# A fused linear attention and mixture of experts: row scatters are no longer ordered behind the early reads of the first two experts

## Chip, cores and metric

One core of a Trainium2 chip. The metric is the device time of one execution in microseconds. The kernel is written in Tile: the program names tiles and operations, and the framework derives from them which instruction has to wait for which. Engine names in the profile: PE is TensorE (matmuls; PEld its weight loads), DVE VectorE, ACT ScalarE, POOL GpSimd, SP SyncE, which here only issues DMAs.

## What is computed

A gated linear recurrence over 768 tokens for 4 x 8 heads of width 48, and behind it a mixture of 8 experts in which every one of the 4 x 768 = 3,072 tokens goes to exactly one expert:

```
f = 1 / (1 + exp(-f_logit))
for t in range(S):                                  # S = 768
    state = f[:, :, t, :, None] * state + einsum('bhd,bhe->bhde', k[:, :, t], v[:, :, t])
    y[:, :, t] = einsum('bhd,bhde->bhe', q[:, :, t], state)
x = y.transpose(0, 2, 1, 3).reshape(3072, 384)
logits = x @ w_gate                                 # (3072, 8)
expert_idx = argmax(logits, axis=1)
gate_w = softmax(logits)[arange(3072), expert_idx]
for e in range(8):                                  # rows of expert e
    y[rows_e] = maximum(x[rows_e] @ w1[e], 0) @ w2[e]   # 384 -> 1024 -> 384
return gate_w[:, None] * y
```

All numbers are float32.

## The kernel before

**Two stages.** The first works through the recurrence in 12 units (NU = 12). A unit is one chunk of 128 tokens of two batches, with all heads. The second goes through the 8 experts, each with its w1 and w2, 1.5 MB each.

**Between the stages lies a buffer in device memory**, `xs`, with a region of rows for each expert. A row has 400 floats (1,600 bytes): the token's 384 values, its number (TOK) and its weight (GATE). As soon as the tokens of a unit are known, each is written into the next free row of its expert. That is a scatter (L189): an indirect DMA issued by POOL, 128 rows at a time, whose row numbers come from a tile `posi`.

**How a row finds its place.** `rows` (L663) multiplies a unit's outputs `ys` with a matrix that both turns them to row layout and gives the gate's logits. `lay` (L688, L693) copies the rows from PSUM to a tile `xr`. Two units at a time form a group, up to units 8 and 9; units 10 and 11 stand alone. For each group a `Route` does: `choose` (DVE, L214 to L222: which expert), `count` (PE, L226 and L227: how many before this one, into `rp`), `place` (DVE, L233 to L251: the row numbers `posi`, read from `rp`), `weigh` (ACT, L254), `fill` (DVE, L258 to L260: the gate's weight into `xr`), and `send` (POOL, the scatters: four for a group of two units, two for a single unit).

**The order of the loop** over n = 1 to 13 (L803) is written out by hand. Within one n the unit `here` = n is scored (L543) and masked (DVE, L549), the unit before it gets its outputs (L571 within the chunk, L592 from the state), and the unit two back is settled (ACT, L633, a copy from PSUM into the single buffer `ys`) and put into rows (L663). While the loop still has units ahead, scatters are handed out two at a time (`sends`, `scatter_some`). Near the end they go out at once: those of units 6 and 7 near the end of n = 10, after `place` and `fill`; those of units 8 and 9 in n = 12; those of unit 10 in n = 12; those of unit 11 in n = 13.

**Early reads.** At n = 10 (NU - 2), before the scatters of units 6 and 7 in program order, `load_rows` reads the first 128 rows of experts 0 and 1 (EARLY = 2) from `xs`: for each, four DMAs of blocks (`load_blocks`, L273) into a tile `xrow` and one (L285) of token numbers and weights into `tg`, all issued by SP. PE begins with these two experts while the last units' routing is still going on: `turn_early` transposes the rows (DVE, L299), `widen` (PE, L316, in three parts: 3, 4 and 1 of 8 blocks, into banks that the trace calls `s`) multiplies with w1, with the relu on ACT (L326) or DVE (L328), and `narrow` (PE, L332, into `yp`) with w2, behind which the results are scaled (L343) and scattered to the output. The rows that are read must have been written by then. Whether the first 128 rows of both experts are full is tested when units 4 and 5 are placed (`settled`, the tile `lack`); if one is not, a general path behind the main program does the rows again. With these inputs it does not run.

**What orders the scatters.** The framework treats `xs` as one tensor: a scatter may write any row, so it would wait for all earlier scatters and reads of `xs`. Between scatters that is switched off: each is declared free of the group "xs" and joins it (`declare_no_dep`, `add_to_no_dep_group`), since no row is written twice. The early reads are in no such group. A read waits for the scatters issued before it, and a scatter issued after the reads waits until they have landed.

**Behind the loop** SP writes padding rows (`load_pads`) and reads the remaining rows of the experts; both come after the last scatters.

Of the kernel before, what the change touches and what calls it, by code (L numbers as in the profile page):

```python
# [19 lines left out]
C = 128  # L20
# [35 lines left out]
BK = 32  # L56
# [6 lines left out]
TOK, GATE, USED, ROW = DM, DM + 1, DM + 2, DM + 16  # L63
# [62 lines left out]
def kernel(  # L126
# [15 lines left out]
    nc = tc.nc  # L142
# [13 lines left out]
    xs = nc.dram_tensor("xs", (ROWS + T, ROW), F32, kind="Internal").ap()  # L156
# [28 lines left out]
    nc.gpsimd.memset(pad, 0.0)  # L185
    nc.gpsimd.memset(pad[:, TOK : TOK + 1], float(FAR))

    def scatter(dst, idx, src, bound, group=None):
        ins = nc.gpsimd.indirect_dma_start(  # L189
            out=dst,  # L190
            out_offset=bass.IndirectOffsetOnAxis(ap=idx, axis=0),
            in_=src,
            in_offset=None,
            bounds_check=bound,
            oob_is_err=False,
        ).ins
        if group:
            tc.declare_no_dep(ins, group=group, reason="no row is written twice")
            tc.add_to_no_dep_group(group, ins)

    class Route:

# [59 lines left out]
        def send(self, chunks):  # L262
            for c in chunks:
                scatter(xs, self.posi[:, c : c + 1], self.xr[:, c, :], ROWS - 1, self.group)
# [4 lines left out]

    def load_blocks(to, rows):  # L270

        for j in range(128 // BK):
            nc.sync.dma_start(  # L273
                to[BK * j : BK * j + BK],
                rows[:, DB * j : DB * j + DB].rearrange("(i c) m -> c i m", c=BK),
            )

    def load_rows(row, count=C):

        rows = xs[ds(row, count)] if not isinstance(row, int) else xs[row : row + count]  # L280
        n, whole = -(-count // C), count // C
        x = rowp.tile([128, TILES * C // BK, DB], F32, name="xrow")[:, 0 : count // BK]
        tg = rowp.tile([128, TILES, USED - TOK], F32, name="tg")[:, 0:n]
        load_blocks(x, rows)
        nc.sync.dma_start(  # L285
            tg[:, 0:whole], rows[0 : whole * C, TOK:USED].rearrange("(t p) r -> p t r", p=C)
        )
        if n > whole:
            nc.sync.dma_start(tg[0 : count - whole * C, whole], rows[whole * C :, TOK:USED])
        return {"n": n, "rows": count, "x": x, "tg": tg}  # L290

    def turn(x, pool=None):

# [47 lines left out]
    def put(x, t, yp, group):  # L341
        ysb = ep.tile([128, DM], F32, name="ysb")
        nc.vector.tensor_scalar(ysb, yp, x["tg"][:, t, 1:2], None, op0=OP.mult)  # L343
        scatter(out, x["dst"][:, t : t + 1], ysb, N - 1, group)
# [13 lines left out]
    def put_half(x, t, h, yp, group):  # L358
        ysb = ep.tile([128, HD], F32, name="ysh")
        nc.vector.tensor_scalar(ysb, yp, x["tg"][:, t, 1:2], None, op0=OP.mult)  # L360
        scatter(out_halves, x["dst2"][:, h : h + 1], ysb, 2 * N - 1, group)
# [30 lines left out]
    def load_expert(e):  # L392

        t = int(e < EARLY)
        x = load_rows(first[e] + t * C, int(FIXED[e]) - t * C)
        if e in RIDE:
            rows = xs[ds(slot(0, RIDE[e], NONE), T)]
            nc.sync.dma_start(x["tg"][C - T :, TILES - 1], rows[:, TOK:USED])
        return x
# [21 lines left out]
    with ExitStack() as st:  # L421
# [46 lines left out]
        whole, ab = slice(0, SEG), (slice(0, HP), slice(HP, SEG))  # L468
# [132 lines left out]
        def added(u):  # L601

            x = units[u]
            x["dp"] = turns("dp", [128, SEG, D])
            for a in range(2):
                for p, h, r in heads():
                    s = HP * a + p
                    nc.tensor.matmul(  # L608
                        x["dp"][r, s],
                        lhsT=x["kn"][:, s, r],  # L610
                        rhs=x["v"][:, a, 2 * p + h],
                        start=s == 0,
                        stop=True,
                        skip_group_check=True,
                    )

        def update(u):

            x = units[u]
            new = wk.tile([128, SEG, D], F32, name="state", bufs=4)  # L620
            last = _bc(x["last"], 2, D)
            if x["old"] is None:
                nc.vector.tensor_copy(new, x["dp"])
            else:
                nc.vector.tensor_tensor(new, x["dp"], x["old"], op=OP.add)
            states[u % 2] = new
            return lambda: nc.gpsimd.tensor_tensor(new, new, last, op=OP.mult)
# [7 lines left out]
        group = {}  # L635
# [167 lines left out]
        for n in range(1, NU + 2):  # L803
# [20 lines left out]
                scatter_some(n)  # L824
            if n == NU - 2:
                soon = [load_rows(first[e]) for e in range(EARLY)]
            if n == 1:
                units[0]["old"] = None
                added(0)
                update(0)()  # L830
# [208 lines left out]
    with ExitStack() as st:  # L1039
# [4 lines left out]
        def quad_rows(q):  # L1044

            x = qp.tile([128, 4, DB], F32, name="qrow")
            quad = {"q": q, "n": 1, "rows": C, "x": x, "second": [None] * 4}
            if q != 0:
                quad["tg"] = qp.tile([128, 1, USED - TOK], F32, name="qtg")
            for g in range(4):  # L1050
                rows = xs[ds(slot(0, 4 * q + g, NONE), T)]
                load_blocks(x[:, g : g + 1], rows)
                if q != 0:
                    nc.sync.dma_start(quad["tg"][g * T : g * T + T, 0], rows[:, TOK:USED])
            return quad
# [85 lines left out]
        for e in range(E):  # L1141
            x, w = rows_of[e], weights[e]
# [32 lines left out]
    with tc.If(todo > 0):  # L1175

        flag = nc.values_load(badi[0:1, 0:1], min_val=0, max_val=1)
        with tc.If(flag > 0):
            with ExitStack() as st:
# [6 lines left out]
                ins = {x: gp.tile([128, S], F32, name=f"g{x}") for x in "qkf"}  # L1186
# [69 lines left out]
        with ExitStack() as st:  # L1256
            bank, narrow_late, psz = tile_pools(st)
            with tc.For_i(0, E) as e:
                w1t = wpool.tile([128, KD, F], F32, name="w1t")
                w2t = wpool.tile([128, NF, DM], F32, name="w2t")  # L1260
                for w, src, by in ((w1t, moe_w1, W1), (w2t, moe_w2, W2)):
                    nc.sync.dma_start(
                        w, src[ds(e, 1)].rearrange("o a b -> (o a) b").rearrange(by, p=128)
                    )
                end = ep.tile([1, 1], I32, name="end", bufs=1)
                nc.sync.dma_start(end, ends_of[0:1, ds(e, 1)])
                rows_to = nc.values_load(end[0:1, 0:1], min_val=0, max_val=ROWS - C)
                nc.sync.dma_start(xs[ds(rows_to, C)], pad)
                with tc.For_i(e * REGION + skip, rows_to, C) as at:
                    x = load_rows(at)  # L1270
                    turn(x)
                    x["hT"] = ep.tile([128, NF, C], F32, name="hT", bufs=1)
                    widen(x, (w1t, w2t), bank, range(NF))
                    narrow_late(x, 0, (w1t, w2t), None)
# [53 lines left out]
```

## Time and profile before

| | |
|---|---|
| six executions | median 400.96 us, 400.43 to 402.29 |
| the profiled execution | 403.07 us; its span from first to last instruction 401.3 us |
| PE busy | 383.6 us (96% of the span) |
| DVE, POOL, ACT busy | 169.6, 116.5, 103.1 us |
| moved by DMA | 95.05 MB, mean 237 GB/s |
| mean granted clock of TensorE | 0.982 |

The profile is one execution, recorded by the hardware. Times in the timeline count from the span's start in microseconds. A timeline row reads: start, length, engine, line, operation, output<-input, shape, number of instructions merged into it, and in brackets how long the engine was idle before it and what ended the wait (inferred from semaphores). `issue` is time in which the profile shows nothing that was waited for. The ends of matmuls are modelled, so a row's end on PE is when the matmuls should be done, and the start of the instruction that reads the result is when the result was handed over.

The first stage lasts until about 138 us, the experts from there to the end; up to 154 us the early rows of experts 0 and 1 are worked on.

### The profile page before, as it was taken

What the parts mean: (1) busy time and instruction counts of PE and PEld (TensorE: products, weight loads), DVE (VectorE), ACT (ScalarE), POOL (GpSimd) and SP (SyncE); (2) the same over time, 40 slices, a digit from 0 to 9 for tenths busy, and PEclk for the clock granted to TensorE, in tenths of its full rate; (3) what the DMA queues carried; (4) which work ended last, traced back from release to release, by engine and by line L of the source; (5) the groups of instructions that cost most, each with busy time, mean ns of one, the idle gap of its engine ahead of it and who ended that gap; (6) DMA issues with size and microseconds to landing.
All of it is one profiled execution on the core that took longest, in us unless ns stands there. A gap on an engine that the chain in (4) does not pass through costs nothing.

```text
span 401.3 us, 7727 instructions
## 1 busy us (share of the span) xinstructions
PE 383.6 (96%) x3062; PEld 270.7 (67%) x3062; DVE 169.6 (42%) x365; ACT 103.1 (26%) x190; POOL 116.5 (29%) x118
## 2 busy tenths in 40 slices
PE   7898999999995999999999999999999999999993
PEld 7887898998985787777555555664556556554452
DVE  6899987989751352203112113113612113111350
ACT  6898877775431100000010010010000000001000
POOL 4378868788517120010100100100100100100011
PEclk9999999999998699999999999999999999999997
DMA  8999657779954147959339899989145349993231
GB/s 283 381 355 371 212 199 265 234 210 343 399 143 163 41 154 211 316 139 305 88 130 353 233 376 392 277 339 339 44 157 187 103 147 394 396 415 137 52 147 42
DMA packets 51516, 95.05 MB, mean 237 GB/s; under 512 B 20824, under 2 KB 40731, under 8 KB 49424
## 3 DMA queue, kind: packets, MB, share of 16 engines
q1 hardware_dynamic: 48016, 84.76, 62.5%
q0 software_dynamic: 3168, 9.64, 6.4%
q8 instruction: 25, 0.41, 0.4%
q14 instruction: 19, 0.16, 0.1%
q10 hardware_dynamic: 288, 0.08, 0.1%
HBM read 79.46 MB, written 15.21 MB: 236 GB/s over the span
## 4 chain that ended last, share of the span: by engine, by line
PE 87%; DMA 3%; DVE 2%; issue 2%; another core or an unknown queue 1%; POOL 1%; ACT 1%; SPq 0%; POOLq 0%; DVEq 0%; ACTq 0%
PE hps L316 27%; PE yps L332 23%; PE yps L1107 7%; PE xp L663 6%; PE s L543 4%; PE yt L571 4%; PE s L316 3%; PE hps L1081 3%; PE yp L332 3%; PE yt L592 3%; DMA f<-in_fu_dram 2%; PE kp L558 2%; PE dp L608 2%; DMA k<-in_ku_dram 1%
## 5 line engine op out<-in xcount | busy, mean ns | idle before, releaser
L316 PE MATMUL hps<-xT,w1t 128*128 128x352 f32 (+2 forms) x384 | 110.1, 447 | 0.0
L316 PEld LDWEIGHTS hps<-xT,w1t 128*128 128x128 f32 x384 | 72.7, 190 | 37.2 <-issue 1.9
L332 PE MATMUL yps<-w2t,hT 128*128 128x384 f32 x288 | 94.4, 487 | 0.0
L189 POOL DMA_INDIRECT out_dram<-ysb,dst x24 | 23.3, 972 | 225.2 <-DVE ysb L343 215.6
L332 PEld LDWEIGHTS yps<-w2t,hT 128*128 128x128 f32 x288 | 54.6, 190 | 38.6 <-issue 1.5
L326 ACT ACTIVATE hT<-hps 128x352 f32<-128x352 f32 (+2 forms) x28 | 13.7, 490 | 200.7 <-PE hps L316 171.9
L328 DVE TENSOR_SCALAR hT<-hps 128x352 f32<-128x352 f32 (+2 forms) x28 | 15.6, 558 | 93.0 <-PE hps L316 93.0
L343 DVE TENSOR_SCALAR ysb<-yps,tg 128x384 f32<-128x384 f32 x22 | 13.6, 618 | 74.4 <-PE yps L332 55.7
L189 POOL DMA_INDIRECT xs<-xr,posi x24 | 33.3, 1388 | 26.9 <-DVE ex L222 12.7
L549 DVE COPY_PREDICATED at<-mpack,s 128x512 f32<-128x512 uint8 x48 | 31.1, 729 | 6.2 <-PE s L543 6.2
L509 POOL TENSOR_TENSOR k<-k,r 128x1024 f32<-128x1024 f32 (+1 forms) x12 | 26.5, 2213 | 19.8 <-ACT r L505 10.4
L491 DVE TENSOR_TENSOR_SCAN sum<-g,cap 128x1032 f32<-128x1032 f32 (+1 forms) x14 | 28.8, 2060 | 3.5 <-ACT g L484 3.5
L663 PE MATMUL xp<-fpack,ys 128*128 128x104 f32 x192 | 26.4, 288 | 4.0 <-ACT ys L633 2.9
L663 PEld LDWEIGHTS xp<-fpack,ys 128*128 128x128 f32 x192 | 23.5, 197 | 6.1 <-ACT ys L633 3.2
L1107 PE MATMUL yps<-qw,hqT 128*32 128x192 f32 (+1 forms) x192 | 27.5, 381 | 0.2 <-issue 0.2
L543 PE MATMUL s<-q,k 64*128 64x128 f32 x384 | 24.7, 278 | 1.7 <-POOL last L527 1.1
L571 PE MATMUL yt<-at,v 128*48 128x128 f32 x384 | 25.1, 276 | 0.0
L543 PEld LDWEIGHTS s<-q,k 64*128 64x128 f32 x384 | 22.4, 188 | 3.6 <-issue 1.5
L571 PEld LDWEIGHTS yt<-at,v 128*48 128x48 f32 x384 | 20.0, 123 | 2.6 <-issue 1.5
L1107 PE MATMUL yps<-w2t,hT 128*32 128x384 f32 x192 | 21.4, 487 | 0.0
L633 ACT COPY ys<-yt 128x512 f32<-128x512 f32 x24 | 12.9, 591 | 17.8 <-PE yt L592 11.8
L532 DVE TENSOR_TENSOR q<-q,g 128x1024 f32<-128x1024 f32 (+1 forms) x14 | 16.5, 1183 | 0.2 <-DMA q<-in_qu_dram 0.2
(114 smaller groups left out, 366.3 us busy)
## 6 DMA issues: line engine op xcount, KB each, us to landing
qw<-in_moe_w_dram SPq DMA_DIRECT2D x16, 1536.0 KB
w1t<-in_moe_w_dram SPq DMA_DIRECT2D x8, 1536.0 KB
w2t<-in_moe_w_dram SPq DMA_DIRECT2D x8, 1536.0 KB
k<-in_ku_dram SPq DMA_DIRECT2D x12, 512.0 KB
q<-in_qu_dram SPq DMA_DIRECT2D x12, 512.0 KB
f<-in_fu_dram SPq DMA_DIRECT2D x11, 512.0 KB
xs<-pad SPq DMA_DIRECT2D x8, 600.0 KB
v<-in_vu_dram SPq DMA_DIRECT2D x12, 384.0 KB
```

The costliest lines, as they stand in the source:

```text
L189: ins = nc.gpsimd.indirect_dma_start(out=dst, out_offset=bass.IndirectOffsetOnAxis(ap=idx, axis=0), in_=src, in_offset=None, bounds_check= ...
L316: nc.tensor.matmul(x["h"][:, f], lhsT=w[0][:, j, b * 128 : b * 128 + 128], rhs=x["xT"][:, j], start=j == 0, stop=j == KD - 1,)
L328: nc.vector.tensor_scalar(to, x["h"], 0.0, None, op0=OP.max)
L332: nc.tensor.matmul(yp, lhsT=x["hT"][:, f, t * C : t * C + C], rhs=w[1][:, f, :], start=f == 0, stop=f == NF - 1,)
L491: nc.vector.tensor_tensor_scan(x["sum"][:, part].rearrange("p s c -> p (s c)"), x["g"][:, part].rearrange("p s c -> p (s c)"), cap[:, part ...
L509: ins = on.tensor_tensor(k, k, units[u]["r"][:, part], op=OP.mult).ins
L532: nc.vector.tensor_tensor(q, q, x["dec"][:, part], op=OP.mult)
L543: nc.tensor.matmul(ps[h][:, p], lhsT=x["k"][r, s], rhs=x["q"][r, s], start=True, stop=True)
L549: nc.vector.copy_predicated(x["at"][:, a, h], _bc(causal, 1, HP), x["ps", a][h])
L571: nc.tensor.matmul(x["yt"][DP * (h ^ a) : DP * (h ^ a) + D, a, p], lhsT=x["v"][:, a, 2 * p + h], rhs=x["at"][:, a, h, p], start=p == 0, st ...
L663: nc.tensor.matmul(xp[:, p], lhsT=x["ys"][:, a, p], rhs=wx[:, p, 0:XW] if a else wx[:, p, E:WX], start=True, stop=True,)
L1107: nc.tensor.matmul(yp[r], lhsT=h[:, f, at : at + T], rhs=w[:, f, cols], start=f == 0, stop=f == NF - 1, skip_group_check=True,)
```

## The change

The scatters of group "xs" that come after the early reads are declared free of them. For this `load_blocks` and `load_rows` hand back their DMA instructions, these are put into a group "early", and `scatter` declares itself independent of that group. Nothing is reordered in the program, no instruction is added, and no buffer changes.

```diff
+    early_reads = []
+
     def scatter(dst, idx, src, bound, group=None):
         ins = nc.gpsimd.indirect_dma_start(
...
         if group:
             tc.declare_no_dep(ins, group=group, reason="no row is written twice")
             tc.add_to_no_dep_group(group, ins)
+        if group == "xs" and early_reads:
+            tc.declare_no_dep(
+                ins,
+                group="early",
+                reason="the early tiles' rows are full, or the general path does them again",
+            )
...
     def load_blocks(to, rows):
 
-        for j in range(128 // BK):
+        return [
             nc.sync.dma_start(
                 to[BK * j : BK * j + BK],
                 rows[:, DB * j : DB * j + DB].rearrange("(i c) m -> c i m", c=BK),
-            )
+            ).ins
+            for j in range(128 // BK)
+        ]
...
-        load_blocks(x, rows)
-        nc.sync.dma_start(
-            tg[:, 0:whole], rows[0 : whole * C, TOK:USED].rearrange("(t p) r -> p t r", p=C)
+        reads = load_blocks(x, rows)
+        reads.append(
+            nc.sync.dma_start(
+                tg[:, 0:whole], rows[0 : whole * C, TOK:USED].rearrange("(t p) r -> p t r", p=C)
+            ).ins
         )
...
-        return {"n": n, "rows": count, "x": x, "tg": tg}
+        return {"n": n, "rows": count, "x": x, "tg": tg, "reads": reads}
...
             if n == NU - 2:
                 soon = [load_rows(first[e]) for e in range(EARLY)]
+                early_reads.extend(ins for x in soon for ins in x["reads"])
+                for ins in early_reads:
+                    tc.add_to_no_dep_group("early", ins)
```

## The prediction

> **What bounds the kernel now.** I read the page first, then the chain of waits, then the timeline from 88 to 160 us engine by engine, then stages. The page says PE 383.6 of 401.3 us: TensorE nearly always has a matmul. Past the kernel's first 43 us, only the stage where the diff works is an exception. This is the chain there (start, length, what):
>
> ```profile
> 118.50 0.22 ACT ex L254
> 118.72 5.94 another core or an unknown queue
> ...
> 125.37 1.41 PE xp L663 x8
> 126.78 0.79 issue
> 127.57 2.00 PE xp L663 x8
> 129.57 0.25 PE s L316
> 129.82 0.52 issue
> ...
> 138.67 5.16 PE yp L332 x16
> ```
>
> From 138.51 (first L332 matmul in the timeline) to the end PE has no gap worth naming: the stage 138:154 below shows 16.00 busy of 16.00. So the end is 138.51 + 262.8 = 401.3, and only what moves 138.51 counts. The stages are start:end, length, busy time of PE, PEld, DVE, ACT, POOL, then granted clock, DMA share, GB/s:
>
> ```profile
> 107.00:118.00 11.00, 10.80 (x170) 9.81 (x160) 6.83 (x31) 4.36 (x11) 0.00 (x0) 1.00 0.76 247
> 120.00:128.00 8.00, 4.24 (x35) 3.91 (x33) 1.03 (x7) 1.07 (x2) 5.98 (x7) 0.97 0.40 154
> 128.00:138.00 10.00, 8.58 (x38) 7.83 (x38) 1.71 (x12) 1.62 (x5) 3.28 (x7) 0.51 0.21 82
> 138.00:154.00 16.00, 16.00 (x87) 11.98 (x87) 9.22 (x38) 0.60 (x1) 3.00 (x3) 1.00 0.45 141
> ```
>
> POOL does nothing from 107 to 118, then scatters without a pause; in those 8 us PE is half idle, and for the next 10 its clock is 0.51. What did PE wait for? The timeline, one line for each end of a hand-over:
>
> ```profile
> 118.93 1.09 PE L592 MATMUL yt<-q,state 48*48 48x128 f32 x32
> 120.19 0.38 PE L227 MATMUL rp<-oh,fpack 128*128 128x16 f32 x2
> 124.73 1.07 ACT L633 COPY ys<-yt 128x512 f32<-128x512 f32 x2 [6.01 <-remote]
> 126.80 0.17 DVE L234 COPY counts<-rp 128x16 f32<-128x16 f32 x1 [7.59 <-PE xp L663]
> 133.36 0.29 DVE L671 TENSOR_REDUCE lg<-xp 128x8 f32<-128x32 f32 x2 [5.04 <-PE s L316]
> ```
>
> L592 ends by its row at 120.02, yet its reader L633 starts at 124.73 (4.71 late); L227 ends at 120.57, its reader L234 starts at 126.80 (6.23); the second L663 group ends at 129.57, its reader starts at 133.36 (3.79). Six us earlier the same hand-overs took 0.13 (L592 to L633, 114.32 to 114.45) and 0.03 (L227 to L234, 114.89 to 114.92), and after the scatters 0.03 again (137.87 to 137.90). Late hand-overs begin with the first of ten back-to-back scatters and end 2.7 us after the start of the last:
>
> ```profile
> 106.07 0.15 POOL L655 MEMSET xr<- 128x56 f32 x1
> 118.89 0.99 POOL L189 DMA_INDIRECT xs<-xr,posi  x1 [12.67 <-DVE ex L222]
> 120.19 0.97 POOL L189 DMA_INDIRECT xs<-xr,posi  x1 [0.30 <-issue]
> ...
> 130.64 0.97 POOL L189 DMA_INDIRECT xs<-xr,posi  x1 [0.30 <-issue]
> ```
>
> Pairs of scatters earlier show it small: L608 ends at 98.81 during one of 97.99 to 99.09, and its reader L625 starts at 99.56, 0.75 late; the L592 beside it takes 1.43 against 1.09 elsewhere. I don't know the mechanism; that scatters cause it is an inference from this coincidence.
>
> **The change, part by part.** No instruction is added. *Removed:* POOL's wait for ten reads (eight L273, two L285; SP issues them from 111.12 to 116.70) before the first scatter of units 6 and 7; the 12.67 us in its row. The label names a DVE step; the wait instructions of L189 run from 116.4, when the reads land. Its data (L251, L260) are ready at 107.74, and the instruction itself carries the wait for these, so it can start at 108.0. The same wait in the scatters of units 8 to 11 is long satisfied: nothing. SP's own 10.6 us wait, before the reads, for scatters already sent, stays; it ends at 110.99 as now. *Moved:* four scatters, each one POOL instruction and 128 rows of 1,600 B, from 118.9 to 108.0. Nothing else of POOL stands behind them but the next scatters. The four of units 8 and 9 (ready at 116.59) no longer queue behind them; the pairs of units 10 and 11 wait for DVE anyway.
>
> *DMA collision.* The moved 4 x 0.205 = 0.82 MB now land while the reads run; at the 401 to 436 GB/s of 102 to 108 us that is 2.0 us, so the reads, used by the transpose L299 at 118.39, may come at 120.4. I price it at nothing, covered: in the chain below the choice ahead of L299 ends after 120.6. Without that cover it costs up to 2.0. Bounds: 0 and 2.0.
>
> *What the old waits cost in all.* With no late hand-over PE would do after 120.57: L316 x18 2.25 (to 122.7), L663 2.03, L316 x24 at 0.117 each 2.8, L226/L227 0.6, L316 x6 0.7, so L332 at 128.8 instead of 138.51: 9.7 us to win at most. DVE's choice (1.42, from 133.36 to 134.78) hides under the 2.8.
>
> *What the new place of the scatters costs.* Not shown by any row, so bounded: by pairs, 0.35 us of PE a pair, five pairs 1.8, gain 7.9; by the train of ten, 9.7 over ten scatters is 0.97 each, gain 0. Between them I take trains of four, nearest to neither, and work out the order of events, with a hold that starts about 1 us into a train and is released between 1.5 us (pairs: 97.99 to 99.56) and 2.7 us (ten: 130.64 to 133.36) after its last scatter begins:
> 1. Train one at 108.0, steps of 1.28, last begins 111.85: release 113.4 to 114.6. PE has queued work until 114.32 (scores, L663, L571, L592), so it loses nothing yet. Two of the four masks L549 (1.3 us) and the choice (L671 to L222, 1.6 of work) are late: L226 starts at 116.3 to 117.5 instead of 114.25. PE idles 2.0 to 3.2.
> 2. Counts 0.64, place and scale 1.67 (114.92 to 116.59), 0.8 to issue (139.49 to 140.30 for the last pair): train two from 119.4 to 120.6, last begins 123.2 to 124.4, release 124.7 to 127.1. PE meanwhile does L663, L571, L592 (4.9), counts, L316 x18 (2.25), until 124.7 to 125.9.
> 3. L633 0.6 after the release, L663 2.03: to 127.3 to 129.7. The pair of units 10 starts 2.5 after the release (place and scale 1.5, issue 1.0), so its hold comes after this result is handed over; the choice, 1.4, runs beside PE's 24 L316, which end at 130.1 to 132.5; then 0.6 and 0.8.
> L332 starts at 131.5 to 133.9, middle 132.7: 5.8 us earlier. Against the profiled execution (403.07, span 401.3 and 1.77 around it) that is 397.3; the median of six runs is 400.96, 2.11 less, so **395.2**, own range 394.0 to 396.4, to 400 where the clock drops for part of it.
>
> *A rule weighed: the clock.* The clock is 0.51 in 128:138, after PE gaps of 2.70 (122.67 to 125.37) and 1.06. The Trainium skill, "TensorE: Matmul & The Clock Gate", Part 1, says a largely idle window of about 3.4 us halves the clock. By that rule step 1's gap just misses a drop; if one came, the half-speed time would be bought as in the profile.
>
> *A rule that speaks against it: the port.* The row: a scatter of 94.65 took 3.03 us beside DVE's scan L491, one of 103.02 beside the masks L549 took 1.03. The Trainium skill, "DMA: Bandwidth & Descriptors", SWDGE vs HWDGE vs iDMA, says DVE locks GpSimd out of writing descriptors in its two-port mode. By the rule, if masks counted, train one would last 13.0 instead of 4.9, its last scatter would begin 6.2 later, and the estimate would be 401.4. From 108 to 118 DVE runs masks and small operations, no scan, so the row's 1.03 holds.
>
> **Rivals.** *The hold disappears* (391.3 to 393.1): split trains act like pairs, or like the single scatters after 145, beside which PE shows no gap. For it: earlier pairs; against it: eight of them still follow each other closely. *It only moves* (400.3 to 401.6): 0.97 a scatter wherever it stands, or a wait I don't see keeps POOL where it is. For it: the count of scatters is the same. *Slower* (402.3 to 406): train one now falls into the recurrence, where every step waits for the one before. If its hold on the masks leaves PE idle before L226 for more than the 3.8 us (2.70 + 1.06) that preceded the drop now, the clock halves for the 10.24 us it stayed down before, 5.1 lost, and reads late by 2.0 no longer have cover: 133.9 + 5.1 + 2.0 = 141.0, 2.5 later than now, 403.5; more holds in the chain than I counted make up the rest. Against it: 2.0 to 3.2 is less than 3.8.
>
> **Chances.** Forecast 0.41, hold gone 0.20, only moved 0.15, slower 0.24. About 0.3% (1.2 us) can be told from no change. Faster: 0.61 plus a little of the third, 0.63; same 0.12; slower 0.25. Range from the second case to the near half of the fourth: 390.8 to 402.8, beside the forecast's own 394.0 to 396.4.
>
> **What would show it.** Right: first scatter of units 6 and 7 near 108 with no long wait; trains of four; L592 to L633 still late near 124, by less; L332 first at 131.5 to 133.9; less time at 0.5 clock. Wrong: the first scatter still at 118; hand-overs prompt with scatters running (then they were never the cause); L299 late and PE waiting for it; a clock under 1 before 125.

## The result, and the profile after

| | before | after |
|---|---|---|
| median of the runs | 401.67 us (39 runs, 399.05 to 403.53) | 398.2 us (18 runs, 395.69 to 400.48) |
| ratio, 95% interval | | 0.9918 (0.9902 to 0.9933) |
| profiled execution, its span | 403.07, 401.3 | 397.74, 395.9 |
| mean granted clock of TensorE | 0.982 | 0.990 |

Faster by 0.8%, some 3.3 us, where 5.8 were forecast. 398.2 lies outside the forecast's own 394.0 to 396.4, inside its "to 400 where the clock drops for part of it" and inside the whole range of 390.8 to 402.8. In the changed kernel's trace the line numbers stand 2 to 12 higher: the scatter is L191, the outputs are L583 and L604, the copy to `ys` L645, the rows L675, `count` L234 and L235, `widen` L328, `narrow` L344.

The timeline of the changed kernel, POOL's scatters and the readers of PE's results:

```profile
107.69 0.99 POOL L191 DMA_INDIRECT xs<-xr,posi  x1 [1.78 <-DVE xr L268]
...
110.54 1.34 DVE L561 COPY_PREDICATED at<-mpack,s 128x512 f32<-128x512 uint8 x2 [0.93 <-PE xp L675]
111.55 0.97 POOL L191 DMA_INDIRECT xs<-xr,posi  x1 [0.30 <-issue]
112.75 0.19 DVE L683 TENSOR_REDUCE lg<-xp 128x8 f32<-128x32 f32 x1 [0.87 <-remote]
...
118.29 0.97 POOL L191 DMA_INDIRECT xs<-xr,posi  x1 [5.77 <-DVE lg L683]
...
122.12 0.97 POOL L191 DMA_INDIRECT xs<-xr,posi  x1 [0.30 <-issue]
124.37 1.07 ACT L645 COPY ys<-yt 128x512 f32<-128x512 f32 x2 [4.82 <-PE yt L604]
```

The train of ten has become two trains of four and a pair, that of unit 10 (the pair of unit 11 stood alone before too). The first train starts where the data are ready, not at 118.9. The second pair of masks L561 starts at 110.54, though its scores end by PE's row at 109.13 and DVE is free from 109.61, and the first L683 starts at 112.75, 0.87 after DVE has become free: results are handed over late, as they were before, but by less. From 118.29 on it is different, as the chain of waits shows (start, length, what):

```profile
119.83 0.96 PE yt L604 x20
120.80 0.31 issue
121.11 0.44 PE yt L604 x5
...
123.00 1.01 issue
124.01 0.27 PE yt L604
...
124.83 3.48 PE s L328 x18
...
134.14 5.16 PE yp L344 x16
```

Here no reader is late: PE itself stands still, for nothing that the profile shows, in the middle of the 32 matmuls of unit 11's L604. They take from 119.76 to 124.28 instead of 1.09. After that the eighteen L328 take 3.63 by PE's timeline instead of 2.25, since the clock is at half (0.65 in 125:126, 0.50 in 126:128). The stages (start:end, length, busy time of PE, PEld, DVE, ACT, POOL, granted clock, DMA share, GB/s):

```profile
107.00:118.00 11.00, 9.92 (x142) 8.88 (x136) 6.09 (x25) 3.87 (x9) 3.91 (x4) 1.00 0.88 310
120.00:128.00 8.00, 5.97 (x54) 4.65 (x47) 1.35 (x9) 1.07 (x2) 3.48 (x6) 0.83 0.25 95
128.00:138.00 10.00, 10.00 (x65) 8.41 (x65) 5.56 (x27) 1.72 (x5) 3.34 (x6) 0.96 0.16 61
```

In 107:118 PE has lost 0.88 of its 10.80 busy time; in 120:128 it has gained 1.73, in 128:138 another 1.42, and the clock there is 0.96 instead of 0.51.

### The profile page after: what moved, and what is told of

Same layout as the page of the kernel before. It is cut to its first block, busy times and chain, and to the rows that moved or that the text cites. A ratio compares the mean times of both kernels' runs of the same rounds, so it can differ in the third digit from the quotient of the medians.

```text
span 395.9 us, 7723 instructions
## 1 busy us (share of the span) xinstructions
PE 380.0 (96%) x3062; PEld 267.3 (68%) x3062; DVE 170.4 (43%) x365; ACT 103.1 (26%) x190; POOL 116.8 (30%) x118
## 4 chain that ended last, share of the span: by engine, by line
PE 86%; DMA 5%; DVE 3%; issue 1%; SPq 1%; ACT 1%; another core or an unknown queue 0%; POOL 0%; POOLq 0%; DVEq 0%; ACTq 0%
PE hps L328 28%; PE yps L344 24%; PE yps L1122 7%; PE xp L675 5%; PE yt L583 4%; PE s L555 4%; PE s L328 3%; PE yt L604 3%; PE hps L1096 3%; PE yp L344 3%; DMA fpack<-c_fpack 2%; PE dp L620 2%; DMA f<-in_fu_dram 2%; PE kp L570 2%; DMA fpack<-in_moe_w_gate_dram 1%
## 5 line engine op out<-in xcount | busy, mean ns | idle before, releaser
L328 PE MATMUL hps<-xT,w1t 128*128 128x352 f32 (+2 forms) x384 | 110.1, 447 | 0.0
L328 PEld LDWEIGHTS hps<-xT,w1t 128*128 128x128 f32 x384 | 72.7, 190 | 37.2 <-issue 1.9
L344 PE MATMUL yps<-w2t,hT 128*128 128x384 f32 x288 | 94.4, 487 | 0.0
L191 POOL DMA_INDIRECT out_dram<-ysb,dst x24 | 23.3, 971 | 224.5 <-DVE ysb L355 216.2
L344 PEld LDWEIGHTS yps<-w2t,hT 128*128 128x128 f32 x288 | 54.6, 190 | 38.6 <-issue 1.5
L191 POOL DMA_INDIRECT xs<-xr,posi x24 | 33.3, 1387 | 22.7 <-DVE hT L340 6.0
L561 DVE COPY_PREDICATED at<-mpack,s 128x512 f32<-128x512 uint8 x48 | 31.2, 729 | 7.2 <-PE s L555 6.2
L555 PE MATMUL s<-q,k 64*128 64x128 f32 x384 | 24.7, 278 | 1.8 <-POOL last L539 1.2
L583 PE MATMUL yt<-at,v 128*48 128x128 f32 x384 | 25.4, 277 | 0.9 <-issue 0.9
L675 PE MATMUL xp<-fpack,ys 128*128 128x104 f32 x192 | 25.4, 283 | 0.4 <-DMA fpack<-in_moe_w_gate_dram 0.2
L555 PEld LDWEIGHTS s<-q,k 64*128 64x128 f32 x384 | 22.4, 188 | 3.7 <-issue 1.5
L675 PEld LDWEIGHTS xp<-fpack,ys 128*128 128x128 f32 x192 | 23.1, 194 | 2.3 <-issue 1.3
L583 PEld LDWEIGHTS yt<-at,v 128*48 128x48 f32 x384 | 20.1, 123 | 3.6 <-issue 2.5
L645 ACT COPY ys<-yt 128x512 f32<-128x512 f32 x24 | 12.9, 591 | 15.3 <-PE yt L604 15.2
```

What stands on the lines that cost most here:

```text
L191: ins = nc.gpsimd.indirect_dma_start(out=dst, out_offset=bass.IndirectOffsetOnAxis(ap=idx, axis=0), in_=src, in_offset=None, bounds_check= ...
L328: nc.tensor.matmul(x["h"][:, f], lhsT=w[0][:, j, b * 128 : b * 128 + 128], rhs=x["xT"][:, j], start=j == 0, stop=j == KD - 1,)
L344: nc.tensor.matmul(yp, lhsT=x["hT"][:, f, t * C : t * C + C], rhs=w[1][:, f, :], start=f == 0, stop=f == NF - 1,)
L555: nc.tensor.matmul(ps[h][:, p], lhsT=x["k"][r, s], rhs=x["q"][r, s], start=True, stop=True)
L561: nc.vector.copy_predicated(x["at"][:, a, h], _bc(causal, 1, HP), x["ps", a][h])
L583: nc.tensor.matmul(x["yt"][DP * (h ^ a) : DP * (h ^ a) + D, a, p], lhsT=x["v"][:, a, 2 * p + h], rhs=x["at"][:, a, h, p], start=p == 0, st ...
```

## The experiments

One length is used for all runs, each time of the one profiled execution: from the first score row of unit 11 on PE (L543 before, L555 after) to the first `narrow` matmul (L332, L344). What comes before it is the same in all kernels, and behind it PE has nothing to wait for but the late reads. The experiments fell on four chips; the third column says which kind, by about what the kernel before took there.

| kernel | from, to | before takes | length |
|---|---|---|---|
| before; again in the fifth run | 107.40, 138.51; 107.91, 138.27 | 401 | 31.1; 30.4 |
| after; again in the sixth run | 107.08, 133.98; 106.64, 134.04 | 401 | 26.9; 27.4 |
| e9, units 6 and 7 spread out | 107.54, 130.88 | 401 | 23.3 |
| e10, one pair at the old place | 107.45, 130.38 | 401 | 22.9 |
| e11, that pair behind unit 10 | 107.15, 129.34 | 401 | 22.2 |
| e7, e8: units 8 and 9 moved away | 107.10, 129.10; 106.70, 128.72 | 401 | 22.0; 22.0 |
| e1 to e4 | 105.88, 126.57 (e1) | 390 | 20.7 in each |

**e1: units 8 and 9 behind unit 11.** The two theories: scatters that run close together hold PE up; or PE is stopped by something else and the scatters only stand beside it.

```diff
-            if sends:
+            if sends and n < NU:
                 scatter_some(n)
...
             if later and n >= NU - 1:
                 settled(*later)
                 later = None
-                scatter_some(NU)
+                if n < NU:
+                    scatter_some(NU)
...
                 if n >= NU:
                     settled(*later)
                     later = None
+                if n == NU + 1:
+                    scatter_some(NU)
```

> The four scatters of units 8 and 9 move from their place near 118.3 to behind the pair of unit 11. Theory (scatters that follow each other closely hold up PE): the L604 of unit 11, which took from 119.76 to 124.3 in the changed kernel, takes its usual 1.1, and the first L344 (narrow) starts near 129.5 (L604 to 120.9, L234 0.4, L328 x18 2.25, L675 2.0, L328 x24 2.8, then 0.6 and 0.8) instead of 133.98. The reads of the remaining rows wait for six scatters in a row and start near 142, which leaves PE about 2.9 idle before the first L328 into hps; the profiled execution 396.1, 1.6 under the changed kernel. Rival one (PE is stopped there by something else, the scatters only stand beside it): L604 still stretched to about 124, L344 near 134, and the end later by the later reads, 399 or more.

390.84, and the kernel before on the same chip 390.2: ratio 1.0021 (1.0011 to 1.003). Neither theory had this: the chip is faster by 11 us for the kernel before. PE's timeline of e1 shows why, already beside the four scatters of units 6 and 7, which ran from 106.50 to 111.31 with the same pauses of 0.30 as elsewhere:

```profile
109.83 1.95 PE L583 MATMUL yt<-at,v 128*48 128x128 f32 x32
...
126.57 5.33 PE L344 MATMUL yp<-w2t,hT 128*128 128x384 f32 x16
```

Nothing stands still, and the masks' scores are handed over 0.01 after PE's row ends, beside the second scatter of the train. On this chip scatters don't hold PE up. The later reads cost PE 0.66 before the first L328 into `hps`.

**e2 and e3: substitutes at the old place.** The kernel of e1, with work on POOL alone (e2, the first part), or the same bytes without POOL (e3, the second).

```diff
+                if n == NU:
+                    nc.gpsimd.tensor_copy(dead[:, 0:4], later[1].xr[:, :, GATE])
+                    for _ in range(14):
+                        nc.gpsimd.memset(dead, 0.0)
...
+                if n == NU:
+                    for c in range(4):
+                        nc.sync.dma_start(xt[c], later[1].xr[:, c, :])
```

> As the one before, with fourteen memsets of a dead tile (about 0.36 each, 5 in all) on POOL at the place near 118.3, behind the same data. If it is scatters that hold up PE: L604 takes 1.1, L344 near 129.5, as without the memsets. If any work on POOL at this place does it: L604 stretched to about 124 as in the changed kernel.

> As the first, with the same 4 x 205 KB written at the place near 118.3 from the same tiles to an unused buffer by four plain DMAs that SP issues, without POOL. If the traffic of the rows is what holds up PE: L604 stretched, by a similar 3 us, L344 near 133. If it is POOL's issuing of scatters: L604 takes 1.1 and L344 starts near 129.5.

391.25 and 390.33, L344 after 20.7 in both. On a chip where even scatters do nothing, this says nothing; e8 has both in one kernel.

**e4: memsets between the scatters**, from n = 10 on.

```diff
             for c in chunks:
                 scatter(xs, self.posi[:, c : c + 1], self.xr[:, c, :], ROWS - 1, self.group)
+                if early_reads:
+                    for _ in range(4):
+                        nc.gpsimd.memset(dead, 0.0)
```

> The changed kernel with four memsets (1.4 together) on POOL behind each scatter from n = 10 on, so that scatters start every 2.7 instead of 1.28. Theory (close succession holds up PE): hand-overs are prompt or late by at most 1 beside each single scatter; L604 takes 1.1 to 2, the first L344 starts at 129.5 to 131.5, though the last scatter of unit 9 now ends at 127.3; the profiled execution 394 to 396. Rival one (something else stops PE): L604 to about 124, L344 at 134. Rival two (each scatter has its fixed price of about 0.9 wherever it stands): L344 near 133 to 134, time as the changed kernel within 1.

399.25, ratio 1.0231 (1.0208 to 1.0254), on the chip with 390. Up to L344 it is the same 20.7 (at 126.64), so that theory isn't touched. What it shows is the price of late scatters: the last one starts at 140.37, the reads of the remaining rows wait for it, and PE waits for them (`widen` is L332 in this kernel):

```profile
149.08 12.46 PE L332 MATMUL hps<-xT,w1t 128*128 128x256 f32 x48 [6.38 <-DVE dst L321]
```

**e5, e6, e7: before, after and e1 side by side**, without a new edit, to see them on one chip.

> The kernel before, unchanged, profiled again: in the first experiments it took 390.2 on their chip against 400 to 403 in the runs of the prediction. If the chip decides whether scatters hold up PE: where this run takes about 390, its L592 beside the ten scatters takes 1.09, the hand-over to L633 is prompt (under 0.2), and the first L332 comes near 126 to 127 instead of 138.5; where it takes about 401, the late hand-overs are there again. If the difference between the chips lies elsewhere (transfers, clock over the whole span), L332 stands near 137 in a run of 390 too and the rest is shorter.

> The changed kernel, unchanged, on the same chip as the kernel before. Theory (the gain is only the hold of the scatters on PE, made shorter): on a chip with 390 for the kernel before the change gives nothing, 389.5 to 391, within 0.3%; on a chip with 401 it gives the 3 us seen, ratio 0.990 to 0.993. Rival (the gain comes from the earlier end of the scatters, thus earlier reads of the remaining rows, and has nothing to do with PE being held): 3 us faster on either chip.

> The first experiment again, beside the two kernels: the four scatters of units 8 and 9 moved behind the pair of unit 11. On a chip with 390: as there, 390.8. On a chip with 401, theory: L604 of unit 11 takes 1.1 instead of 4.5, the first L344 starts near 129.5, 2 us faster than the changed kernel; rival one: L604 stretched to 124 and no faster.

This chip took 401.2 for the kernel before. e5 took 404.25, with its late hand-overs at other points than in the first profile: the first scatter starts 1.3 later, L592 is signalled only 1.0 late, and it is the L316 behind L663 that stand still, in seven pieces from 124.78 to 134.12. e6 took 398.86, ratio 0.9934 (0.9905 to 0.9963): the change gains here about what it gained at first (2.6 by the ratio, 3.3 then; the intervals overlap). e7 took 394.17, ratio 0.9827 (0.9767 to 0.9886), 4.7 under e6 on the same chip; 2 were expected. PE's timeline of e7:

```profile
111.05 1.41 PE L583 MATMUL yt<-at,v 128*48 128x128 f32 x21
112.74 0.27 PE L583 MATMUL yt<-at,v 128*48 128x128 f32 x1 [0.29 <-issue]
113.47 0.84 PE L583 MATMUL yt<-at,v 128*48 128x128 f32 x10 [0.46 <-issue]
...
119.94 1.09 PE L604 MATMUL yt<-q,state 48*48 48x128 f32 x32
...
121.43 2.25 PE L328 MATMUL s<-xT,w1t 128*128 128x128 f32 x18
...
129.10 5.33 PE L344 MATMUL yp<-w2t,hT 128*128 128x384 f32 x16
...
146.30 3.91 PE L328 MATMUL hps<-xT,w1t 128*128 128x256 f32 x17 [1.13 <-DVE dst L317]
```

With the four scatters gone from 118.3, L604 is whole again, the clock stays at 1.00, and L344 starts at 129.10, where 129.5 was expected for the theory and 134 for its rival. The train of units 6 and 7 is still there and still costs: L583 in three pieces, so that it ends at 114.31 instead of 113.00, 1.3 late; the lengths, 22.0 against the 20.7 of the other chip, say the same. The reads take back 1.13. That the hold comes with the scatters is now shown, on this kind of chip.

**e8: both substitutes at once**, the edits of e2 and e3 together.

> The kernel with the four scatters of units 8 and 9 moved behind unit 11, and at their old place near 118.3 both substitutes at once, behind the same data: fourteen memsets on POOL (5 together) and four plain DMAs by SP that write the same 4 x 205 KB to an unused buffer. On a chip where scatters hold up PE (kernel before about 401). If neither POOL work nor this traffic as such holds up PE: L604 of unit 11 takes 1.1 and the first L344 starts near 129.1, as without the substitutes. If either does: L604 stretched and L344 near 132 to 134. On a chip with 390 it says nothing.

393.82, where the kernel before took 400.78. The timeline, PE, POOL and SP (lines stand 2 higher than in e7):

```profile
117.35 1.82 SPq L876 DMA_DIRECT2D xt<-xr  x4
117.53 5.86 POOL L879 MEMSET dead<- 128x320 f32 x14
119.55 1.09 PE L606 MATMUL yt<-q,state 48*48 48x128 f32 x32
...
128.72 5.33 PE L346 MATMUL yp<-w2t,hT 128*128 128x384 f32 x16
```

Neither 5.86 of work on POOL nor the same 0.82 MB from the same tiles holds PE up. What is left is what only a scatter does: POOL issuing an indirect DMA, or the writes to scattered rows. Which of the two it is wasn't tried.

**e9: units 6 and 7 spread out.** The kernel of e7, with the four memsets of e4 behind each scatter of units 6 and 7 only.

> Units 8 and 9 moved behind unit 11 as before, and the four scatters of units 6 and 7 apart: four memsets (1.65) behind each, so that they start every 3 us from 107.7 to 116.8 instead of every 1.28; POOL has nothing else to do until 124. On a chip with 401 for the kernel before. Theory (close succession holds up PE): L583 of unit 10 in one piece, 1.95 instead of 3.3 with two pauses, the L604 behind it near 113.0 instead of 114.24, the first L344 near 127.9 instead of 129.1, and 393.0 against 394.2. Rival (each scatter has a fixed price): pauses spread over the stage, L344 at 129.1 within 0.3 and 394.2 within 0.5. On a chip with 390: no difference to 390.8.

Both were wrong. 396.42, ratio 0.9867 (0.982 to 0.9913), 2.6 slower than e8 on the same chip; three of the four runs took 396.4 to 396.6, one 393.95. The timeline (lines 4 higher than in e7), and two stages of the same execution (columns as above):

```profile
113.38 1.09 PE L608 MATMUL yt<-q,state 48*48 48x128 f32 x32
114.21 0.97 POOL L192 DMA_INDIRECT xs<-xr,posi  x1 [0.39 <-issue]
115.63 1.07 ACT L649 COPY ys<-yt 128x512 f32<-128x512 f32 x2 [2.35 <-PE rp L236]
116.27 2.67 PE L679 MATMUL xp<-fpack,ys 128*128 128x104 f32 x16 [1.24 <-ACT ys L649]
118.87 2.92 PE L587 MATMUL yt<-at,v 128*48 128x128 f32 x32
```

```profile
115.00:117.00 2.00, 0.76 (x7) 0.74 (x7) 1.20 (x7) 1.07 (x2) 1.65 (x5) 1.00 0.61 187
118.00:120.00 2.00, 2.00 (x17) 1.80 (x18) 0.88 (x5) 0.68 (x3) 1.83 (x7) 0.50 0.28 103
```

The first two scatters, at 108.15 and 111.17, delay nothing (0.01 at each hand-over), where in the train the second pair of scores was late by 1.4. So distance does help there. But the third, alone, falls on the end of L608, whose reader starts 1.16 late just where PE has nothing else to do: 1.24 idle, and then a clock of 0.50 that makes 2.03 into 2.67 and 1.95 into 2.92. "Close together" isn't the whole condition: one scatter is enough if the result it meets is the next that PE waits for. In the one run of 393.95 the mean clock was 0.998 against 0.990 to 0.995, so there the drop was missing; that it makes most of the 2.5 between the runs is an inference from this.

**e10: one pair at the old place.** Unit 8 stays near 118.3, unit 9 goes behind unit 11.

```diff
-                scatter_some(NU)
+                scatter_some(0 if n == NU else NU)
```

> Only the pair of unit 9 goes behind unit 11; the pair of unit 8 stays near 118.3. On a chip with 401 for the kernel before. Theory (a pair costs PE little, 0 to 0.75, a train of four 3.4): L604 of unit 11 takes 1.1 to 1.9, the first L344 starts at 129.1 to 129.9; the reads of the remaining rows begin 2.6 earlier than with both pairs moved, so that PE's gap of 1.13 before the first L328 into hps goes, and the time is 393.1 to 393.9. Rival (0.97 for each scatter): L344 at 131.0, time 395. On a chip with 390: 390.2, as the kernel before.

393.81, ratio 0.9817 (0.9782 to 0.9852), a time as expected; but L604 took 1.98 and L344 came at 130.38, where at most 1.9 and 129.9 were expected, and 131.0 for the rival. PE's timeline:

```profile
120.33 1.01 PE L604 MATMUL yt<-q,state 48*48 48x128 f32 x21
121.66 0.65 PE L604 MATMUL yt<-q,state 48*48 48x128 f32 x11 [0.32 <-issue]
```

A pair costs 0.9 (22.9 against 22.0), four in a row cost 4.9 to 5.4 (26.9 and 27.4 against 22.0), the clock drop among it: far more than twice. PE has no gap before `hps` here, which pays the 0.9 back.

**e11: that pair behind unit 10** instead, where POOL was idle; the added line stands behind the `settled` of n = 12 and 13.

```diff
-                if n < NU:
-                    scatter_some(NU)
...
+                    scatter_some(0 if n == NU else NU)
```

> The pair of unit 8 goes behind the pair of unit 10 (near 124, POOL was idle there from 126.4), the pair of unit 9 behind that of unit 11. On a chip with 401 for the kernel before. Theory (what a scatter meets decides: beside L604 and L583 of the units it stops PE, beside the L328 and L344 of the early experts it costs little): L604 of unit 11 takes 1.1, the first L344 starts at 129.1 to 129.5 although four scatters run in a row from 124 to 129, and without PE's gap of 1.13 before hps the time is 393.0 to 393.5. Rival (four in a row stop PE wherever they stand): hand-overs of L675 and L234 late by 1.4 to 4, L344 at 130.5 to 133, time 394.5 to 397. On a chip with 390: 390.2.

393.3, ratio 0.9797 (0.9745 to 0.9849), L344 at 129.34: as expected. Of the kernels tried it has the lowest ratio, though its interval covers those of e7 and e10. The train of four from 124.19 to 129.00 isn't free of holds: L235 is handed over 1.26 late, and the narrow matmuls come in two parts with 0.17 between them. But PE had L328 and the first L344 to do in the meantime:

```profile
128.59 0.91 PE L328 MATMUL s<-xT,w1t 128*128 128x128 f32 x6
129.34 2.75 PE L344 MATMUL yp<-w2t,hT 128*128 128x384 f32 x8
130.03 0.17 DVE L242 COPY counts<-rp 128x16 f32<-128x16 f32 x1 [2.90 <-PE s L328]
132.25 2.85 PE L344 MATMUL yp<-w2t,hT 128*128 128x384 f32 x8 [0.17 <-DVE hT L340]
```

**e12: the cost by itself**, in the dense stage of the experts.

```diff
                 narrow_late(x, t, w)
+                if e in (2, 3):
+                    for c in range(4):
+                        scatter(probes[c], x["dst"][:, t : t + 1], pad, N - 1, f"probe{c}")
+                if e in (4, 5):
+                    for c in range(4):
+                        nc.scalar.dma_start(plain[e - 4, t, c], pad)
```

> The cost by itself, in the stage of the experts: units 8 and 9 moved behind unit 11, and in experts 2 and 3 four extra scatters in a row of 128 rows to unused buffers behind every scatter of results; in experts 4 and 5 four plain DMAs of the same size instead, issued by ACT. The result is not touched. On a chip with 401 for the kernel before. If close scatters stop PE anywhere: each of the six trains costs 1.3 to 3.4, experts 2 and 3 last 8 to 20 longer. If they do so only beside the units' short matmuls that wait for one another: PE without gaps in experts 2 and 3, the whole 394 to 395. The plain DMAs: nothing. On a chip with 390: nothing anywhere.

404.31, where the kernel before took 401.64 and the kernel of e7, on another chip of the kind, 394.17. The result scatters and the extra ones joined into trains of fifteen, 209.69 to 228.55 and 240.65 to 259.51. PE and DVE beside the first of them, in e12 (lines 2 higher than in e7):

```profile
218.91 15.64 PE L330 MATMUL hps<-xT,w1t 128*128 128x384 f32 x48
...
228.28 0.56 DVE L342 TENSOR_SCALAR hT<-hps 128x384 f32<-128x384 f32 x1 [8.55 <-PE hps L330]
```

and in e7, without them:

```profile
218.69 15.64 PE L328 MATMUL hps<-xT,w1t 128*128 128x384 f32 x48
...
222.84 0.56 DVE L340 TENSOR_SCALAR hT<-hps 128x384 f32<-128x384 f32 x1 [3.32 <-PE hps L328]
```

PE's 48 matmuls take 15.64 in both. But the second of their results (the first that DVE takes) is read at 228.28 instead of 222.84, 5.3 after its matmuls end, and the next ones at 231.1 and 231.2. So the hold is there in the dense stage too, but costs these matmuls nothing, because PE has other banks to fill: of the expectations the second had PE without gaps there, but neither had a time of 404.31. PE's one gap in these experts, 4.91 at 265, is a wait for weights (`qw`), which SP issued at 262.05 instead of 254.12; behind it the clock is at 0.50 until about 275.6, and the other 42 matmuls take 8.03, where in e7 all 48 take 5.36. SP, in e12:

```profile
254.66 0.46 SPq L303 DMA_DIRECT2D tg<-xs  x1
258.38 0.69 SPq L412 DMA_DIRECT2D tg<-xs  x1
262.05 1.54 SPq L1079 DMA_DIRECT2D qw<-in_moe_w_dram  x2
```

and in e7:

```profile
250.93 0.46 SPq L301 DMA_DIRECT2D tg<-xs  x1
252.53 0.34 SPq L410 DMA_DIRECT2D tg<-xs  x1
254.12 1.54 SPq L1077 DMA_DIRECT2D qw<-in_moe_w_dram  x2
```

For the same steps SP takes 7.4 beside the end of the train and just behind it, in e7 3.2: SP is slowed there too, and that is 4.2 of the 7.9 by which the weights are issued late. How the rest is shared between late signals and the 4.9 MB of extra writes at a DMA share of 0.98 isn't told apart. The plain DMAs left no gap of PE behind.

## Why the prediction was right, and where it was off

*What bounds the kernel* was right: late hand-overs beside scatters, not the data of units 6 and 7 or the reads. e7 and e8 show that it is the scatters. What I couldn't see in one profile is that it depends on the chip: where the kernel before takes 390, "the hold disappears" was, by e1's prompt hand-overs, already the case before the change; the kernel before wasn't profiled there. The changed kernel itself didn't run there; its gain there wasn't measured.

*The first scatter at 108.0*: 107.69, with the unit's own start 0.3 earlier in this execution. Right. The scatters beside the masks took 0.97 to 0.99, as the row of 1.03 said, not 3.03, so the weighed rule of the port didn't bear on masks. ("No scan" from 108 to 118 was not quite so: DVE has a small one, L235, 0.24 at 115.15; no scatter stood beside it.)

*Step 1*, L226 at 116.3 to 117.5: it came at 115.09 (L234). The release was put at 113.4 to 114.6; the two L683 started at 112.75 and 113.52. PE's loss was put at 2.0 to 3.2; busy time fell by 0.88, and train one costs 1.3 in e7. Mis-sized, on the safe side.

*Step 2*, train two from 119.4 to 120.6 and released at 124.7 to 127.1: it began at 118.29, and L604 came to its end at 124.28, 2.2 after its last scatter began, inside the 1.5 to 2.7 I had. What failed is the sentence "PE meanwhile does L663, L571, L592 (4.9), counts, L316 x18 (2.25), until 124.7 to 125.9". I had taken the hold to delay only the signal of a result. It also stops PE within L604, so the counts and the eighteen L328 came after the release, not beside it: 2.25 uncovered, and 3.63 because the standstill was followed by half clock. The first profile had shown such stops in small: its L316 stood still four times, for 0.2 to 0.5, between 129.8 and 133.2, and the L592 beside a pair took 1.43. I had kept a clock drop only as an edge of the range.

*Step 3*, L332 at 131.5 to 133.9: 133.98. From the release to L332 I had 6.8; from the end of L604 it took 9.7. The hand-overs beside unit 10's pair were prompt (0.01), as assumed. The release itself came 0.4 to 2.8 earlier than I had it, since train two began earlier, and that made good about half of the 2.9 lost. Two errors of opposite sign, so the interval almost held for the wrong reason.

*The sum.* The profiled execution was put at 397.3 and took 397.74, which is luck: L344 came 1.3 after the middle of the forecast, and what follows it took 261.9 instead of 262.8. And the step "the median of six runs is 400.96, 2.11 less" failed: the profile after lies 0.46 under its median, not 2.11 over it. I carried the excess of one execution of before over as if it belonged to both kernels. Where it came from isn't shown: e5, with a length of 30.4 instead of 31.1, lay still further over the median of its chip, 3.05, so the length alone doesn't tell it. By lengths the change is worth 3.0 to 4.2 (30.4 to 31.1 against 26.9 to 27.4), the forecast 5.8 (31.1 against 132.7 - 107.4 = 25.3). The medians say 3.5.

*The rivals.* "It only moves" had more in it than I gave it: train two alone costs 4.9 to 5.4 (against 22.0), where the ten cost 9.7 to 10.4 (against 20.7). "Slower", with train one stopping PE until the clock drops, didn't come, since PE's loss there was small; that this can happen is seen in e9, after 1.24 idle and not the 3.8 I had asked for. *The DMA collision* cost nothing: L311 (L299) ran at 119.22 instead of 118.39, and the L328 that use it started at 124.67.

## What to carry to other kernels

A wait on an engine off the critical path can be worth removing although nothing waits for that engine, if its work in the wrong place disturbs the others; but then the new place decides, so look at what each scatter will stand beside. Place them where PE has independent matmuls and spare banks (e11), not where its next step waits for its last result (e9), and not in long trains, beside which SP's loads come late (e12). And run the kernel before on more than one chip before a gain is believed to be the kernel's own: here 11 of 401 us were the chip's.

## What the runs showed of the hardware

- On three chips PE's results reach their readers late beside scatters (up to 6.2 in e12, where a row ends at 224.88 and ACT reads it at 231.13), on a fourth by 0.01 at the same places, with scatters of the same 0.97 and the same pauses. What differs between the chips, and the path on which the signals are held, stay open. One thing recurs: where PE is stopped within a group, it goes on after steps of some 0.7 or twice that (121.11, 121.86, 122.56 and 124.01 in the changed kernel; 130.34, 131.07, 131.78 and 133.20 before; 112.74 and 113.47 in e7), not at the scatters' step of 1.28. All executions here were recorded; whether recording has a part in it wasn't tried.
- The clock fell to 0.50 after little idleness: 1.24 in one piece in e9, and some 2.0 in four pieces between 120.8 and 124.0 in the changed kernel; the half clock began 1.2 and 1.3 after the end of the idleness (at 117.47 and 125.30). By the traces' clock records every stretch of half clock that ended before the kernel did lasted 3.41 or a whole multiple of it (3.41 in these two, 10.24 in the kernel before, 13.65 in e5). The Trainium skill, "TensorE: Matmul & The Clock Gate", Part 1, speaks of an idle window of about 3.4 us; by the measurement, less than half of that was enough, and my bound of 3.8 for the rival was too high. Idle time alone doesn't decide it: in the kernel before, 1.49 of the 3.41 from 120.75 to 124.16 were idle, and the clock stayed at 1.00 until 127.58. What else counts isn't shown.
